# The boundary of a batch in a fused attention and feed-forward kernel: the last head pair's transpose by DMA, with other work laid behind it

## Chip, cores and metric

The kernel runs on one core of a Trainium2 chip. The metric is the device time of one execution in microseconds (us). Engines are called as in the profile: PE is TensorE (matmuls; PEld its weight loads), DVE is VectorE, ACT is ScalarE, POOL is GpSimd, SP is SyncE, whose queue issues most of the DMAs here.

## What is computed

Attention with a hash mask, and behind it a gated feed-forward block with a gated residual. Cut to what matters:

```python
# attention: batch 4, 8 heads, 768 tokens, head size 64; proj is 64 x 6
q_bits = (q @ proj > 0); k_bits = (k @ proj > 0)          # 6 bits of hash
mask   = bucket(q_bits)[:, :, :, None] == bucket(k_bits)[:, :, None, :]
attn   = softmax(where(mask, q @ k.T / 8, -1e9))
x      = heads side by side(attn @ v)                     # 3072 x 512
# feed-forward, width 1536
ffn    = (gelu(x @ w_gate) * (x @ w_val)) @ w_out
out    = x + sigmoid(x @ w_res) * ffn
```

## The kernel before, in words

**Units.** There are four batches (`b` = 0 to 3). The eight heads of a batch are taken as four pairs (`p` counts pairs over all batches, `hp` within one, `hi` is the head in the pair). The 768 tokens are six tiles of 128.

**Slots.** Attention of one batch takes 36 slots, nine a pair. In a slot (loop at L617) PE computes scores for 1024 columns (L381) into one of two PSUM buffers with the tag "sp" (two banks each), ACT takes the exponential of them (L386), and two slots later PE multiplies them with the values (L355, "av"). When a head is done, `finish` (L299) divides by the row sums on DVE (L306, L307) and writes `x_tok`, tokens on the partitions. Every head from the second batch on starts with a preset: a memset on DVE (`opened`, L321), one small matmul (`preset`, L329) and a copy on DVE (`repeat`, L333). Slot numbers for those three are at L512 to L516.

**Feed-forward of the batch.** It needs `x` with features on the partitions (`x_sb`), in four blocks of 128 features, one per pair. `finish` turns most pairs by a DMA transpose that SP issues (L310). The last pair of each batch (and the last two of the first batch) is turned on PE by `x_turn` (L335): six transposes through an identity matrix (L339) and a copy out of PSUM. `gate_val` (L404) then runs 12 blocks of hidden features; for each it makes eight matmuls with `wg` and eight with `wv` (L400: four blocks `kk` of `x`, each as 512 and 256 columns), a Gelu on ACT (L419) and a product on DVE (L420, into `hh`). The two "sp" buffers hold the two sums. In the first batch alone the sums of block 0 are begun over three pairs before the fourth pair is turned (`begun`).

**The output rows.** `project(b)` (L426) is a generator: for each of six token tiles four matmuls with `wr` (L432, PSUM tag "r", Tanh on ACT), twelve with `wo` (L446, PSUM tag "f"), two DVE instructions (L450, L453) and the store (L455). It is run a step (one matmul) at a time between the scores and the values of the next batch's slots. L624 sets the pace: 3 steps ahead, and `NMM - HELD` = 96 - 13 = 83 steps done by the last slot. The 13 that are held back run at the end of the batch (L641 to L645): four before the last values, five behind them, then `x_turn`, then the rest.

**The hash of the next batch.** `hashed` (L518) computes the hash products of two pairs, q and k, in fp32 (L205, PSUM tag "r"), `tokens` transposes them on DVE, `bits` writes the signs, and `turn` (L248) sends the result through a DMA transpose on SP. For the second and third batch `hashed` runs whole in `gate_val` after block 0 (L589); for the first it runs in two parts, three quarters behind `x_turn` and a quarter behind block 0 (L416, L639).

**What orders the work.** The program is written in the order in which each engine is to run it, and nothing reorders it. Each engine takes its own instructions in that order, and so does SP's queue. Work is attached by hand: `side_pe` and `side_work` to slots, `gv_work` to blocks of `gate_val`. A PSUM or SBUF buffer with a tag is handed to its next user when all that used it before are done.

Of the kernel before, what the change touches and what calls it, by code (L numbers as in the profile page):

```python
# [10 lines left out]
BF16 = mybir.dt.bfloat16  # L11
# [6 lines left out]
def kernel(  # L18
# [12 lines left out]
    nc = tc.nc  # L31
    B, H, S, D = q.shape
# [3 lines left out]
    P = 128  # L36
    KM = DMODEL // P
    KF = DFF // P
    T = S // P
    HP = H // 2  # L40
# [15 lines left out]
    hh_pool = ctx.enter_context(tc.tile_pool(name="hh", bufs=1))  # L56
# [242 lines left out]
    def finish(p, hi):  # L299
        b, hp = divmod(p, HP)  # L300
        if hp == 0 and hi == 0:
            x_tok[b] = x_pool.tile([P, HP, T, 2 * D], BF16, tag="x_tok", name="x_tok")
            x_sb[b] = x_pool.tile([P, HP, T, P], BF16, tag="x_sb", name="x_sb")
        o = av.pop((p, hi))
        rec = sm_pool.tile([P, T], FP32, tag="rec", name="rec")
        nc.vector.reciprocal(rec, o[:, 0:T, D])  # L306
        nc.vector.tensor_mul(x_tok[b][:, hp, :, hi * D:(hi + 1) * D], o[:, 0:T, 0:D],  # L307
                             rec.unsqueeze(2).to_broadcast([P, T, D]))
        if hi == 1 and hp < HP - (2 if b == 0 else 1):
            nc.sync.dma_start_transpose(out=x_sb[b][:, hp],  # L310
                                        in_=x_tok[b][:, hp].rearrange("p t n -> p (t n)"))

# [20 lines left out]
        nc.vector.tensor_copy(o[:, 0:T, :], o[:, T:T + 1, :].to_broadcast([P, T, D + 1]))  # L333

    def x_turn(b, hp):  # L335
        pt = mm_ps.tile([P, T, P], BF16, tag="f", name="pt") if b == 0 else \
            sc_ps.tile([P, T, P], BF16, tag="sp", name="pt")
        for t in range(T):
            nc.tensor.transpose(pt[:, t, :], x_tok[b][:, hp, t, :], ident)  # L339
        if b == 0 and hp == HP - 1:  # L340
            nc.scalar.activation(x_sb[b][:, hp, 0:2], pt[:, 0:2], AF.Copy)
            nc.vector.tensor_copy(x_sb[b][:, hp, 2:T], pt[:, 2:T])
        else:
            nc.vector.tensor_copy(x_sb[b][:, hp], pt)
# [46 lines left out]
    hidden = {}  # L391
# [9 lines left out]
                                 start=(kk == 0), stop=(kk == KM - 1))  # L401
        return sp

    def gate_val(b, begun=None):  # L404
        hh = hh_pool.tile([P, KF, S], BF16, tag="hh", name="hh")
        hidden[b] = hh
        for m in range(KF):
            ps = []
            for i, w in enumerate((wg, wv)):
                if m == 0 and begun:  # L410
                    sp = gv_mm(b, m, w, KM - 1, KM, begun[i])
                else:
                    sp = gv_mm(b, m, w, 0, KM)
                ps.append(sp)
                if m == 0 and begun and i == 1:
                    hashed((HP, HP + 1), 3, 4)  # L416
                if w is wg:
                    gt = g_pool.tile([P, S], BF16, tag="gt", name="gt")
                    nc.scalar.activation(gt, sp[:, 0:S], AF.Gelu)  # L419
            nc.vector.tensor_mul(hh[:, m, :], gt, ps[1][:, 0:S])  # L420
            for piece in gv_work.pop((b, m), []):
                piece()

# [2 lines left out]
    def project(b):  # L426
        hh = hidden[b]
        for t in range(T):
            last = b == B - 1 and t == T - 1
            rps = mm_ps.tile([P, DMODEL], FP32, tag="r", name="rps")  # L430
            for kk in range(KM):
                nc.tensor.matmul(rps, x_sb[b][:, kk, t, :], wr[:, kk, :],  # L432
                                 start=(kk == 0), stop=(kk == KM - 1))
                if kk == KM - 1:
                    th = g_pool.tile([P, DMODEL], FP32, tag="th", name="th")
                    nc.scalar.activation(th, rps, AF.Tanh, scale=0.5)  # L436
                yield
            o = o_pool.tile([P, DMODEL], FP32, tag="o", name="o")
            for k0, k1 in ((0, 3), (3, 4)) if last else ((0, KM),):
                cs = slice(k0 * P, k1 * P)  # L440
                if b < B - 1:
                    fps = mm_ps.tile([P, DMODEL], FP32, tag="f", name="fps")
                else:
                    fps = sc_ps.tile([P, DMODEL], FP32, tag="sp", name="fps")
                for m in range(KF):
                    nc.tensor.matmul(fps[:, cs], hh[:, m, bass.ts(t, P)], wo[:, m, cs],  # L446
                                     start=(m == 0), stop=(m == KF - 1))
                    if m < KF - 1:
                        yield
                nc.vector.scalar_tensor_tensor(o[:, cs], th[:, cs], 1.0, fps[:, cs],  # L450
                                               op0=ALU.add, op1=ALU.mult)
                o3 = o[:, cs].rearrange("p (k n) -> p k n", n=P)
                nc.vector.scalar_tensor_tensor(o3, o3, 0.5, x_tok[b][:, k0:k1, t, :],  # L453
                                               op0=ALU.mult, op1=ALU.add)
                nc.sync.dma_start(out_t[b, t][:, cs], o[:, cs])  # L455
            yield

# [30 lines left out]
    NSLOT = HP * NCH  # L490
    LAST = NPAIR * NCH
    LAG = 2
    HELD = 13
    AHEAD = 3
    side_pe, side_work = {}, {}

# [6 lines left out]
    def gv(b, m, *pieces):  # L503
        gv_work.setdefault((b, m), []).extend(pieces)
# [5 lines left out]


    for p in range(HP, NPAIR):  # L512
        for hi, s in enumerate((9 * p - 1, 9 * p + 4)):
            at(s - 2, lambda p=p, hi=hi: opened(p, hi))
            pe(s, lambda p=p, hi=hi: preset(p, hi))
            at(s, lambda p=p, hi=hi: repeat(p, hi))  # L516

    def hashed(ps, i0=0, i1=4):  # L518
        jobs = [(p, side) for p in ps for side in range(2)]
        for i in range(i0, i1):  # L520
            hash_mm(jobs, (i % 2,), (i // 2,))
# [55 lines left out]
    for b in range(B - 1):  # L577
        s0, p0 = b * NSLOT, (b + 1) * HP
        xs = [(p0 + i, side) for i in range(2) for side in range(2)]
        ys = [(p0 + 2 + i, side) for i in range(2) for side in range(2)]  # L580
        for j, (x, y) in enumerate(zip(xs, ys)):
            at(s0 + 24 + 2 * j, lambda x=x: tr(*x))
            at(s0 + 25 + 2 * j, lambda x=x: cast(*x, nc.gpsimd))
            if j < 2:
                at(s0 + 32 + 2 * j, lambda y=y: tr(*y))
            loads(s0 + (6 if b == 0 else 2) + 4 * j, (x[0], "qk"[x[1]]))
            loads(s0 + (22 if b == 0 else 18) + 3 * j, (y[0], "qk"[y[1]]))
        if b > 0:
            gv(b, 0, lambda p0=p0: hashed((p0, p0 + 1)))  # L589
        gv(b, 0, lambda p0=p0: tokens((p0, p0 + 1), True))  # L590
        for m, x in zip((0, 1, 2, 4), xs):
            lay(b, m, x)
        gv(b, 3, lambda y=ys[2]: tr(*y))
        gv(b, 5, lambda y=ys[3]: tr(*y))
        for m, y in zip((5, 5, 6, 6), ys):
            gv(b, m, lambda y=y: cast(*y, nc.gpsimd))
        gv(b, 6, lambda p0=p0: hashed((p0 + 2, p0 + 3)))
        gv(b, 7, lambda p0=p0: tokens((p0 + 2, p0 + 3), True))
        for m, y in zip((7, 8, 9, 10), ys):
            lay(b, m, y)  # L600
# [7 lines left out]
    def mlp_mm(n):  # L608
        while mlp and n > 0:
            try:  # L610
                next(mlp[0])
                n -= 1
                done[0] += 1
            except StopIteration:
                mlp.pop(0)

    for s in range(LAST):  # L617
        p, c = divmod(s, NCH)
        b, slot = divmod(s, NSLOT)
        cur = scores(p, c)  # L620
        for piece in side_pe.pop(s, []):
            piece()
        if b >= 1:
            mlp_mm(AHEAD + (slot + 1) * (NMM - HELD - AHEAD) // NSLOT - done[0])  # L624
        pending.append(cur)
        while len(pending) > LAG:
            values(*pending.pop(0))
        for piece in side_work.pop(s, []):
            piece()
        if slot == NSLOT - 1:  # L630
            begun = None
            values(*pending.pop(0))
            if b == 0:
                nc.scalar.activation(table, warm[:, 0:1], AF.Gelu)
                begun = [gv_mm(0, 0, wg, 0, KM - 1)]
                values(*pending.pop(0))
                begun.append(gv_mm(0, 0, wv, 0, KM - 1))
                x_turn(b, HP - 1)
                hashed((HP, HP + 1), 0, 3)  # L639
            else:  # L640
                mlp_mm(4)  # L641
                flush()
                mlp_mm(5)
                x_turn(b, HP - 1)
                mlp_mm(NMM)  # L645
            done[0] = 0
            gate_val(b, begun)
            mlp.append(project(b))
    assert not side_pe and not side_work and not gv_work
    for _ in mlp[0]:  # L650
# [31 lines left out]
```

## Time and profile before

| | |
|---|---|
| median of 3 runs | 346.91 us (346.67 to 347.25) |
| profiled execution, its own time | 346.94 us |
| its span, first to last instruction | 345.2 us |
| PE busy | 334.8 us, 97% |
| ACT, DVE, POOL busy | 206.6, 192.7, 86.0 us |
| DMA | 42.5 MB, mean 123 GB/s |
| granted TensorE clock | 1.0 |

How to read the profile. A timeline line has the start in us from the span's beginning, the duration, engine, line of the code, operation, what it writes and reads, shape and count; lines that follow each other and are alike are merged. "Idle before" in brackets is how long the engine had nothing to do, with what released it. Matmuls are pipelined and each record's end is modelled, so a matmul's cost to PE is the distance from its start to the next one's start, which is less than the duration in the record. Some matmul records are missing (a merged line with x7 where eight must be). Stretches of this profile: the first batch's attention ends at about 47 us, the slots of the second, third and fourth batch lie at about 84 to 126, 164 to 206 and 244 to 286 us, and each is followed by its `gate_val`; the last batch's output rows end the span.

### The profile page before, as it was taken

Reading aid. Unit: us, or ns where it says so; the run is one execution under the profiler, and the core shown is the slowest. Engines: PE = TensorE matmul, PEld = TensorE weight load, DVE = VectorE, ACT = ScalarE, POOL = GpSimd, SP = SyncE. Lnnn points to the kernel's source line nnn. Section 1 sums busy time; section 2 is a strip of 40 time slices with the busy share of each in tenths; the row PEclk is TensorE's granted clock in tenths of the full one; section 3 lists DMA queues with packets and bytes.
Section 4 is the critical chain, followed back from the end, with each engine's and each line's share of the span. In section 5 each row is a group of like instructions: output and inputs, shape, how many; then the busy total and the mean of one; then the engine's idle time right before and its main releaser. Section 6 shows DMA issues by size and latency. Waiting matters only on the chain.

```text
span 345.2 us, 7578 instructions
## 1 busy us (share of the span) xinstructions
PE 334.8 (97%) x3076; PEld 204.8 (59%) x3124; DVE 192.7 (56%) x405; ACT 206.6 (60%) x231; POOL 86.0 (25%) x162
## 2 busy tenths in 40 slices
PE   7999999999999999999999999999999999999995
PEld 4667665655666655555666665556566665656443
DVE  6877757755343965757345675747344445343343
ACT  3889973226999962224999992222898994323220
POOL 4779940344055000260054100143030000000000
PEclk9999999999999999999999999999999999999999
DMA  7929999949567623427467542725431221000012
GB/s 237 375 49 238 250 265 196 156 80 227 145 142 225 186 85 78 92 47 139 102 160 211 191 103 84 137 48 92 92 89 43 55 55 61 3 0 0 32 62 91
DMA packets 69572, 42.50 MB, mean 123 GB/s; under 512 B 47905, under 2 KB 66593, under 8 KB 69537
## 3 DMA queue, kind: packets, MB, share of 16 engines
q1 hardware_dynamic: 63120, 36.77, 41.4%
q0 software_dynamic: 6336, 5.24, 10.1%
q8 instruction: 24, 0.39, 0.5%
q14 instruction: 12, 0.09, 0.1%
q10 hardware_dynamic: 80, 0.00, 0.0%
HBM read 29.36 MB, written 6.29 MB: 103 GB/s over the span
## 4 chain that ended last, share of the span: by engine, by line
PE 90%; ACT 4%; DVE 2%; issue 1%; DMA 1%; SPq 0%; DVEq 0%; ACTq 0%
PE sp L400 36%; PE fps L446 17%; PE sp L381 16%; PE av L355 9%; PE rps L432 6%; ACT e L386 4%; PE hs L205 3%; PE pt L259 2%; DMA ld<-in_q_dram 1%; DVE nat L224 0%; PE pt L339 0%; PE hs L234 0%; DVE ht L215 0%; PE av L329 0%; DVE o L453 0%
## 5 line engine op out<-in xcount | busy, mean ns | idle before, releaser
L386 ACT ACTIVATE e<-sp 128x1024 bf16<-128x1024 f32 x144 | 143.8, 1027 | 14.9 <-PE sp L381 9.7
L419 ACT ACTIVATE gt<-sp 128x768 bf16<-128x768 f32 x48 | 38.9, 810 | 95.2 <-PE sp L400 95.2
L381 PE MATMUL sp<-aug,aug 71*128 71x256 bf16 (+1 forms) x384 | 86.1, 325 | 1.1 <-ACT e L386 0.6
L446 PE MATMUL fps<-wo,hh 128*128 128x512 bf16 (+2 forms) x277 | 74.2, 369 | 0.9
L420 DVE TENSOR_TENSOR hh<-gt,sp 128x768 bf16<-128x768 bf16 x48 | 45.8, 954 | 52.4 <-PE sp L400 50.9
L400 PE MATMUL sp<-x_sb,wg 128*128 128x256 bf16 (+1 forms) x374 | 69.9, 325 | 0.6
L355 PEld LDWEIGHTS <-e 128*128 128x128 bf16 x1152 | 53.3, 97 | 28.9 <-issue 1.2
L400 PE MATMUL sp<-x_sb,wv 128*128 128x512 bf16 (+1 forms) x375 | 69.9, 325 | 0.5
L355 PE MATMUL av<-va,e 128*128 128x65 bf16 x1152 | 58.7, 193 | 0.2
L400 PEld LDWEIGHTS <-wg 128*128 128x128 bf16 x384 | 37.0, 98 | 26.3 <-issue 2.1
L400 PEld LDWEIGHTS <-wv 128*128 128x128 bf16 x384 | 37.6, 98 | 24.8
L446 PEld LDWEIGHTS <-hh 128*128 128x128 bf16 x300 | 27.5, 97 | 23.2
L381 PEld LDWEIGHTS <-aug 71*128 71x128 bf16 x384 | 29.4, 97 | 10.9 <-issue 2.2
L281 POOL TENSOR_TENSOR v<-ldv 128x384 f32<-128x384 f32 x16 | 16.0, 998 | 66.2 <-DMA ldv<-in_v_dram 66.0
L184 POOL TENSOR_SCALAR nat<-ld 128x768 bf16<-128x768 f32 (+1 forms) x16 | 13.0, 810 | 75.7 <-DMA aug<-nat 73.7
L194 DVE STREAM_TRANSPOSE t<-ld 128x768 f32<-128x768 f32 (+1 forms) x34 | 30.8, 913 | 1.2 <-DMA ld<-in_q_dram 1.2
L450 DVE SCALAR_TENSOR_TENSOR o<-th,fps 128x512 f32<-128x512 f32 (+2 forms) x25 | 16.6, 665 | 24.8 <-PE fps L446 19.1
L432 PE MATMUL rps<-wr,x_sb 128*128 128x512 bf16 x90 | 26.8, 378 | 0.5
L306 DVE RECIPROCAL rec<-av 128x6 f32<-128x6 f32 x32 | 6.1, 192 | 34.8 <-PE av L355 31.1
L333 DVE COPY av<-av 128x390 f32<-128x390 f32 x24 | 13.5, 564 | 19.2 <-PE av L329 19.1
L436 ACT ACTIVATE th<-rps 128x512 f32<-128x512 f32 x24 | 14.3, 594 | 16.5 <-PE rps L432 16.5
L224 DVE TENSOR_SCALAR nat<-htp 32x72 bf16<-32x72 f32 x96 | 21.9, 229 | 1.8
(61 smaller groups left out, 205.9 us busy)
## 6 DMA issues: line engine op xcount, KB each, us to landing
ldv<-in_v_dram SPq DMA_DIRECT2D x16, 384.0 KB, 5.3
out_dram<-o SPq DMA_DIRECT2D x23, 256.0 KB, 2.1
ld<-in_q_dram SPq DMA_DIRECT2D x15, 384.0 KB, 5.3
ld<-in_k_dram SPq DMA_DIRECT2D x15, 384.0 KB, 5.1
wg<-in_moe_w_gate_dram POOLq DMA_DIRECT2D x4, 384.0 KB, 7.8
wv<-in_moe_w_val_dram POOLq DMA_DIRECT2D x4, 384.0 KB, 9.7
wo<-in_moe_w_out_dram POOLq DMA_DIRECT2D x3, 512.0 KB, 6.3
wr<-in_moe_w_res_dram POOLq DMA_DIRECT2D x1, 512.0 KB, 12.7
```

The source lines that it names most:

```text
L194: nc.vector.transpose(t32[p, side][:, sl].rearrange("p c h n -> p (c h n)"), raw[p, side][:, sl].rearrange("p c d -> p (c d)"))
L224: engs[a % len(engs)].tensor_scalar(nat_of(x)[32 * a:32 * a + 32, :, D:D + NBITS], ht[32 * j:32 * j + 32, :, NBITS * a:NBITS * (a + 1)], 0 ...
L281: nc.gpsimd.tensor_add(v3, vs[:, :, 0:3, :], vs[:, :, 3:6, :])
L355: nc.tensor.matmul(av[p, hi][:, qt, :], e[:, off:off + P], va[:, hi, jt, 0:D + 1], start=first, stop=(p >= HP and jt == T - 1), skip_group ...
L381: nc.tensor.matmul(sp[:, off:off + nq * P], ks[0:KA, hi * T + jt, :], qs[0:KA, hi * T + qt0:hi * T + qt0 + nq, :], start=True, stop=True)
L386: nc.scalar.activation(e, sp, AF.Exp, scale=float(ALPHA))
L400: nc.tensor.matmul(sp[:, c0:c1], w[:, kk, bass.ts(m, P)], xs[:, kk, c0:c1], start=(kk == 0), stop=(kk == KM - 1))
L419: nc.scalar.activation(gt, sp[:, 0:S], AF.Gelu)
L420: nc.vector.tensor_mul(hh[:, m, :], gt, ps[1][:, 0:S])
L432: nc.tensor.matmul(rps, x_sb[b][:, kk, t, :], wr[:, kk, :], start=(kk == 0), stop=(kk == KM - 1))
L446: nc.tensor.matmul(fps[:, cs], hh[:, m, bass.ts(t, P)], wo[:, m, cs], start=(m == 0), stop=(m == KF - 1))
L450: nc.vector.scalar_tensor_tensor(o[:, cs], th[:, cs], 1.0, fps[:, cs], op0=ALU.add, op1=ALU.mult)
```

## The change

Five edits belong together.

1. For the second and third batch the last pair, too, is turned by the DMA transpose in `finish`; `x_turn` is left for the first batch and the last.
2. Block 0 of `gate_val` is begun over three pairs in every batch (12 of its 16 matmuls).
3. 16 steps of `project` are held back instead of 13, which is one whole output row, and the generator's steps are cut differently: the two DVE instructions and the store of a row now come with the first step of the next row, not with the row's last step. At the end of the second and third batch the order is: four steps, the last values, the 12 begun matmuls, the other 12 steps, half of the next hash, the rest of block 0's gate sum, the rest of its value sum, the other half of the hash. In the last batch, which has no next hash, `x_turn` stands behind the 12 begun matmuls, then nine steps, the rest of block 0 and three steps.
4. `x_turn` writes into the PSUM buffer "r" in the last batch, and its copy is shared between ACT and DVE there.
5. Presets move by one slot: 9p instead of 9p - 1 for a pair that is not the first of its batch, and 9p + 5 instead of 9p + 4 for the second head.

```diff
@@ finish
-        if hi == 1 and hp < HP - (2 if b == 0 else 1):
+        if hi == 1 and (0 < b < B - 1 or hp < HP - (2 if b == 0 else 1)):
             nc.sync.dma_start_transpose(out=x_sb[b][:, hp],
@@ x_turn
-        pt = mm_ps.tile([P, T, P], BF16, tag="f", name="pt") if b == 0 else \
-            sc_ps.tile([P, T, P], BF16, tag="sp", name="pt")
+        pt = mm_ps.tile([P, T, P], BF16, tag="f" if b == 0 else "r", name="pt")
...
-        if b == 0 and hp == HP - 1:
+        if hp == HP - 1:
@@ gate_val
-    def gate_val(b, begun=None):
-        hh = hh_pool.tile([P, KF, S], BF16, tag="hh", name="hh")
-        hidden[b] = hh
+    def gate_val(b, begun, beside):
...
-                if m == 0 and begun:
+                if m == 0:
                     sp = gv_mm(b, m, w, KM - 1, KM, begun[i])
...
-                if m == 0 and begun and i == 1:
-                    hashed((HP, HP + 1), 3, 4)
+                if m == 0 and i == 1:
+                    beside()
...
+            if m == 0:
+                hidden[b] = hh_pool.tile([P, KF, S], BF16, tag="hh", name="hh")
@@ project
-                    if m < KF - 1:
-                        yield
+                    yield
...
-            yield
@@
-    HELD = 13
+    HELD = 16
@@
-        for hi, s in enumerate((9 * p - 1, 9 * p + 4)):
+        for hi, s in enumerate((9 * p - (p % HP == 0), 9 * p + 5)):
@@
-        if b > 0:
-            gv(b, 0, lambda p0=p0: hashed((p0, p0 + 1)))
@@ end of a batch
             values(*pending.pop(0))
+            ps = (HP * (b + 1), HP * (b + 1) + 1)
             if b == 0:
...
             else:
                 mlp_mm(4)
                 flush()
-                mlp_mm(5)
-                x_turn(b, HP - 1)
-                mlp_mm(NMM)
+                begun = [gv_mm(b, 0, w, 0, KM - 1) for w in (wg, wv)]
+                if b < B - 1:
+                    mlp_mm(NMM)
+                    hashed(ps, 0, 2)
+                    gate_val(b, begun, lambda: hashed(ps, 2, 4))
+                else:
+                    x_turn(b, HP - 1)
+                    mlp_mm(HELD - 7)
+                    gv(b, 0, lambda: mlp_mm(NMM))
+                    gate_val(b, begun, lambda: mlp_mm(3))
```

More of the change, by code (lines that the diff above doesn't have):

```diff
@@ L419, in gate_val @@
                     nc.scalar.activation(gt, sp[:, 0:S], AF.Gelu)
-            nc.vector.tensor_mul(hh[:, m, :], gt, ps[1][:, 0:S])
+            if m == 0:
+                hidden[b] = hh_pool.tile([P, KF, S], BF16, tag="hh", name="hh")
+            nc.vector.tensor_mul(hidden[b][:, m, :], gt, ps[1][:, 0:S])
             for piece in gv_work.pop((b, m), []):
@@ L630 @@
         if slot == NSLOT - 1:
-            begun = None
             values(*pending.pop(0))
+            ps = (HP * (b + 1), HP * (b + 1) + 1)
             if b == 0:
@@ L638 @@
                 x_turn(b, HP - 1)
-                hashed((HP, HP + 1), 0, 3)
+                hashed(ps, 0, 3)
+                gate_val(b, begun, lambda: hashed(ps, 3, 4))
             else:
@@ L642 @@
                 flush()
-                mlp_mm(5)
-                x_turn(b, HP - 1)
-                mlp_mm(NMM)
+                begun = [gv_mm(b, 0, w, 0, KM - 1) for w in (wg, wv)]
[8 more added lines that the diff above has]
+                    gate_val(b, begun, lambda: mlp_mm(3))
             done[0] = 0
-            gate_val(b, begun)
             mlp.append(project(b))
```

## The prediction

> **What bounds the kernel now.** First the busy shares and the slices, then what PE waited for, then PE's timeline at the ends of the batches.
>
> ```profile
> PE 334.8 (97%) x3076; PEld 204.8 (59%) x3124; DVE 192.7 (56%) x405; ACT 206.6 (60%) x231; POOL 86.0 (25%) x162
> ...
> PE   7999999999999999999999999999999999999995
> ...
> PEclk9999999999999999999999999999999999999999
> ```
>
> PE is full from the second slice on, at full clock. PE's waits come to four lines, all in the first 47 us; asked for the stretch from 84 us to the end, the view is empty. That view passes over short gaps, so I went through the distances between matmul starts: 216 ns after a 512-column matmul, 108 after 256 columns, 29 in a row of "av". From 84 us on only three gaps are longer for a reason other than a missing record: 0.12 us before the preset at 108.92, 0.14 us before the one at 189.14 (both wait for the memset that stands on DVE behind a row's two instructions), and 0.08 us before `x_turn` at 207.76. So the time is the sum of what PE is given, and only 0.34 us of stalls are there to be removed. This is the end of the second batch:
>
> ```profile
> 125.28 0.38 PE L432 MATMUL rps<-wr,x_sb 128*128 128x512 bf16 x1
> 125.50 0.81 PE L446 MATMUL fps<-wo,hh 128*128 128x512 bf16 x3
> 126.14 0.41 PE L355 MATMUL av<-va,e 128*128 128x65 bf16 x8
> 126.39 1.24 PE L446 MATMUL fps<-wo,hh 128*128 128x512 bf16 x5
> 127.47 0.50 PE L339 MATMUL pt<-ident,x_tok 128*128 128x128 bf16 x6
> 127.80 1.03 PE L446 MATMUL fps<-wo,hh 128*128 128x512 bf16 x4
> 128.66 1.46 PE L400 MATMUL sp<-x_sb,wg 128*128 128x512 bf16 x8
> 129.96 1.46 PE L400 MATMUL sp<-x_sb,wv 128*128 128x512 bf16 x7
> 131.36 1.51 PE L205 MATMUL hs<-t,projw 128*32 128x192 f32 x32
> 132.80 0.39 PE L400 MATMUL sp<-x_sb,wg 128*128 128x512 bf16 x1
> ```
>
> Read starts, not durations: the five matmuls at 126.39 cover exactly the time in which DVE makes `x_tok` (it ends at 127.38); nothing is lost here that the change could fill.
>
> **Removed: twelve transposes.** In the lines above the six cost 127.80 - 127.47 = 0.335 us, 56 ns each. Twice that is 0.67 us, and with them goes the 0.08 us wait at 207.76. DVE's copies (L344, 0.56 us) go as well, which is worth nothing: DVE is free there.
>
> **Added: the hash in two pieces.** Whole, as above, it costs PE 94 ns to begin (131.36 less the last matmul's start, 131.155, and its 109 ns), and 1.44 us until 132.80. The first batch shows pieces: three quarters from 50.09 to 51.21, so 1.115 us for six of eight rounds, 0.163 us a round within a piece. The end of a piece costs more, 0.25 us between the last round and the next bf16 matmul. Half a hash is 1.115 - 2 x 0.163 = 0.79, and 0.09 to begin: 0.88. Two halves are 1.77 against 1.53: 0.23 us more, twice: **0.46 us**. This is a real price, since PE has no idle time to hide it.
>
> **Moved at no price on PE.** The 12 begun matmuls, the held-back steps and the presets are the same matmuls elsewhere, with the same distances. Three steps fewer per batch in the slots shorten these by 0.65 us (3 x 0.216) and lengthen the end by as much. ACT doesn't come to limit the slots: when it is behind, its exponentials follow each other in 0.91 us (between 84 and 88 us), and the shortest slot is 1.11 us. The later presets remove the two waits, 0.26 us: for the second head of the third pair, DVE's row now begins early in slot 21 (0.8 us in) and ends with the memset 2.3 us in, and the preset runs 2.9 us in. I laid out all slots in this way. The tightest are `repeat` in slot 14 behind a row's two instructions (ready 0.4 us ahead of its values) and the preset of slot 35 (its memset 0.45 us ahead). If such a cover is gone the price is some tenths of a us a batch. A row's two instructions leave PSUM "f" late by a step, but the four "r" steps of the next row (0.86 us) and a slot of scores and values lie ahead of its next use.
>
> **Added: the transpose on SP.** On its queue it stands behind the store of the fifth row and the load of v, and ahead of the sixth row's store and of the hash's transposes, which come 3 us and more later; nothing late hangs on it but `x_sb`. Its start: in the second batch the last values end 0.65 us sooner, at 125.74; DVE is then just through the fifth row (two instructions of 0.69, from 124.48 to 125.86), so L306 and L307 run from 125.95 to 126.73; SP followed such an end by 0.08 us in this trace. Issue at 126.81. What covers it: 1.95 us of begun matmuls (12, 0.325 a pair), 12 x 0.216 = 2.59 of steps, 0.88 of hash: PE asks for the fourth pair at 125.74 + 5.42 = 131.16. So the transpose has **4.35 us** to land.
>
> ```profile
> x_sb<-x_tok SPq DMA_TRANSPOSE x11, 4.2
> ...
> DMA to landing us min/median/max: 2.7/4.2/6.3
> ```
>
> The first number is the median from issue to landing, the second line the spread. The issues at 257.20, 267.66 and 278.16, with no load about them, took 2.7 to 2.8, and so did that at 187.36; the longer ones had loads just before them (that of 117.82, 5.4, behind a k load at 117.30). Here the v load is issued by 123 and lands in 3.4 (the row at 125.58), at some 126; the store of 256 KB goes out at 125.9 and lands in 2.1, at 128. I take 2.8 to 3.2, landing at 129.6 to 130.0, and keep 2.7 and 5.4 as ends: no stall, or 1.05 us a batch.
>
> The Trainium skill, VectorE: DVE Perf Modes, sections "The three transpose paths" and "Rules for kernel authors", speaks against this edit: 390 ns for a 128x128 transpose on TensorE, 1309 on the DMA's crossbar, and TensorE is to be used where PSUM is a good place for the result. By these figures six tiles would be an estimated 2.3 us on PE and 7.9 by DMA, the removal would save 4.7 us and the transposes would come 3.5 us late, twice. The trace has 0.335 us and 2.7 to 5.4 us for the six, and the measurement decides.
>
> **The waits in block 0.** Gelu's turn decides when PE may begin block 1. In the first batch, from the end of the gate sum at 51.54 to block 1's first matmul at 52.60, it took 1.06 us with PE waiting. In the second and third batch PE has 0.33 + 0.88 = 1.21 us to do in that time: no wait. In the last batch it has 0.33 + 3 x 0.216 = 0.97: **0.09 us lost**. The table that Gelu needs is loaded well ahead (126.31 to 127.59 in the second batch); in the last batch the new copy on ACT (0.38) may stand before that load (1.28), and still both end 0.6 us before Gelu's data. There DVE's share of the copy waits for ACT's, as at 50.62 in the first batch: both are through in 1.2 us, and nine steps (1.94 us) cover them. DVE's chain in block 0 (L420 0.95, L215 0.60, four L224 0.23 each) ends 0.5 us before its next product.
>
> **Sum**, against the profiled execution of 346.94 us (span 345.2 and 1.7 around it): -0.67 - 0.08 - 0.26 + 0.46 + 0.09 = **-0.46 us**. That execution lies 0.03 above the median of the runs, so 346.91 - 0.46 = **346.45**, -0.13%. About 0.2% (0.7 us) is what a measurement can tell from no change, and I forecast less than that.
>
> **Rivals.**
>
> *The transpose is late.* It decides from 4.35 us between issue and landing, or if DVE ends `x_tok` late. For it: the median of 4.2 is close. Against it: the rows above 4.2 had other loads in the queue, and here the last one is done. At 5.4 us: 2 x 1.05 = 2.1 more, 348.5; at 4.8, half of a us a batch, 347.4. Slower.
>
> *The begun matmuls wait for the transpose.* They stand behind it in the program and read another part of the same tile. Were the order kept by whole tiles, PE would wait from 125.74 to 129.6: 3.9 us a batch, 354.2. Against it: `x_tok` was written at 28.12 (L307) while a transpose that reads another pair of that tile (issued 22.51) landed only at 28.80.
>
> *The edits cost less than I count.* If the second piece of the hash is nearly free and Gelu's turn is hidden, only the gains are left: 0.67 + 0.08 + 0.26 = 1.0 us, 345.9. Against it: the 0.25 us at the end of each piece stands at every hash of the trace.
>
> *The DMA replaces nothing in effect.* If the presets wait again, at other slots, the sum is -0.67 - 0.08 + 0.46 + 0.09 = -0.2: 346.7, inside the forecast.
>
> **Chances.** The forecast with its small variants (346.1 to 346.9) has 0.64; the late transpose 0.13; the begun matmuls held 0.03; the cheaper edits 0.17; unforeseen waits in the slots 0.03, up to 1 us a batch. From these: faster by over 0.2% (below 346.2) 0.25, within 0.2% 0.62, slower 0.13. The range of 345.8 to 347.4 takes in the forecast, the gains alone, and the transpose half a us late.
>
> **What would show it.** In the changed profile: no L339 at the ends of the second and third batch; 16 + 16 records of L205 there with four matmuls between them, each piece 0.88 us; the first fourth-pair matmul starting right at the end of the first piece; landings of 2.7 to 3.2; a gap of 0.09 before block 1 in the last batch; no gap before presets. I am wrong if PE's waits list a DMA `x_sb`, if block 0's first matmuls start 3 us after the last values, or if a gap appears at a `repeat`.

## The result

The changed kernel takes 347.40 us (median of 22 runs, 346.84 to 348.05), the kernel before 347.06 in the same session (22 runs, 346.27 to 347.32). The ratio is 1.0014, 95% interval 1.0007 to 1.0020: a small loss where a small gain was forecast. The profiled execution of the changed kernel took 347.61 us with a span of 345.9.

The end of the second batch on PE, changed kernel (start, duration, engine, line, what is written and read, count; compare the ten lines in the prediction):

```profile
125.29 0.41 PE L354 MATMUL av<-va,e 128*128 128x65 bf16 x8
125.54 1.14 PE L399 MATMUL sp<-x_sb,wg 128*128 128x512 bf16 x6
126.51 1.14 PE L399 MATMUL sp<-x_sb,wv 128*128 128x512 bf16 x6
127.49 2.75 PE L445 MATMUL fps<-wo,hh 128*128 128x512 bf16 x12
130.17 0.86 PE L205 MATMUL hs<-t,projw 128*32 128x192 f32 x16
130.96 0.50 PE L399 MATMUL sp<-x_sb,wg 128*128 128x512 bf16 x2
131.29 0.49 PE L399 MATMUL sp<-x_sb,wv 128*128 128x512 bf16 x2
131.71 0.86 PE L205 MATMUL hs<-t,projw 128*32 128x192 f32 x16
```

and SP's queue in the same place:

```profile
125.64 0.36 SPq L453 DMA_DIRECT2D out_dram<-o  x1
126.55 1.22 SPq L310 DMA_TRANSPOSE x_sb<-x_tok  x1
```

Every start follows from the one before: no wait in this stretch. The transpose of 126.55 landed 2.75 us later, at 129.30; PE asked for it at 130.96. What the change was written to do, it does. So the loss lies elsewhere, and it is found by cutting the span at PE's own marks: a batch's slots (from its first score matmul to its last "av"), the rest of the batch (from there to the last matmul of `gate_val`), and the end (from the last matmul with `wo` to the end of the span). They are worked out from the traces, in us, from start to start of matmuls. The first column is a difference, what the prediction's own sum says of changed less before; the others are lengths. The second profile is that of the first experiment below:

| stretch | forecast change | before | changed | changed, second profile |
|---|---|---|---|---|
| slots, second batch | -0.77 | 43.61 | 42.85 | 42.85 |
| rest, second batch | +0.54 | 36.48 | 37.04 | 37.04 |
| slots, third batch | -0.79 | 43.63 | 43.34 | 42.85 |
| rest, third batch | +0.46 | 36.57 | 37.04 | 37.04 |
| slots, fourth batch | -0.65 | 43.47 | 42.82 | 42.82 |
| rest, fourth batch | +0.74 | 33.40 | 34.48 | 34.46 |
| end | 0 | 4.30 | 4.63 | 4.67 |

All that the prediction priced is there to within some 0.02 us. Two lines are off in both profiles, the rest of the last batch by 0.33 and the end by 0.35; a third, the slots of the third batch, in one profile and not in the other. The first 48 us, where loads come in, differ by 0.5 us between the two profiles of the changed kernel alone and are left out.

**The last batch.** Products of `gate_val` on DVE before:

```profile
299.70 0.95 DVE L420 TENSOR_TENSOR hh<-gt,sp 128x768 bf16<-128x768 bf16 x1 [1.65 <-PE sp L400]
302.30 0.95 DVE L420 TENSOR_TENSOR hh<-gt,sp 128x768 bf16<-128x768 bf16 x1 [1.65 <-PE sp L400]
```

and in the changed kernel, with the PE matmul that waits for the second one:

```profile
302.28 0.95 DVE L419 TENSOR_TENSOR hh<-gt,sp 128x768 bf16<-128x768 bf16 x1 [1.65 <-PE sp L399]
305.25 0.95 DVE L419 TENSOR_TENSOR hh<-gt,sp 128x768 bf16<-128x768 bf16 x1 [2.02 <-PE sp L399]
306.26 1.46 PE L399 MATMUL sp<-x_sb,wv 128*128 128x512 bf16 x8 [0.18 <-DVE hh L419]
```

Products come every 2.60 us, this one after 2.97. The wait that stands before it on DVE's sequencer had ended at 304.84; in the blocks around it the product starts 0.045 us after the end of that wait, here 0.41. PE's distance at 306.26 is 0.35 us too long. POOL has no work in this part.

**The end.** After the last store SP waits for everything that is still open, two semaphores an instruction, some 0.06 to 0.07 us for each instruction, in an order that is the same in all traces. SP's loads, stores and transposes take eight completion semaphores in turn. Before, the last store had the seventh in the order and landed at 343.82, with one instruction of those waits left behind it. In the changed kernel, two DMAs on, it has the first in the order: it landed at 344.14 and seven more instructions of waits stood behind it, until 345.00. SP's waits for stores from 342 us on, before and changed (us in total, times, longest):

```profile
SPq L677 <- DMA out_dram<-o: 0.7, 2, 0.6
```

```profile
SPq L679 <- DMA out_dram<-o: 1.1, 1, 1.1
```

Before, SP stops at the last two stores one after the other, late in the order; in the changed kernel it stops once, at the head of the order.

### The profile page after: what moved, and what is told of

It reads as the page before. It is cut to its first block, busy times and chain, and to the rows that moved or that the text cites. A ratio compares the mean times of both kernels' runs of the same rounds, so it can differ in the third digit from the quotient of the medians.

```text
span 345.9 us, 7597 instructions
## 1 busy us (share of the span) xinstructions
PE 337.9 (98%) x3112; PEld 204.4 (59%) x3112; DVE 191.5 (55%) x403; ACT 206.9 (60%) x232; POOL 86.1 (25%) x162
## 4 chain that ended last, share of the span: by engine, by line
PE 89%; ACT 5%; DVE 3%; issue 1%; DMA 1%; SPq 0%; DVEq 0%; ACTq 0%
PE sp L399 36%; PE fps L445 18%; PE sp L380 15%; PE av L354 8%; PE rps L431 5%; ACT e L385 4%; PE hs L205 3%; PE pt L259 2%; DMA ld<-in_q_dram 1%; DVE o L451 1%; DVE o L448 1%; DVE nat L224 0%; PE hs L234 0%; DVE ht L215 0%; DVE hh L419 0%
## 5 line engine op out<-in xcount | busy, mean ns | idle before, releaser
L445 PE MATMUL fps<-wo,hh 128*128 128x512 bf16 (+2 forms) x300 | 79.5, 370 | 0.0
L399 PE MATMUL sp<-x_sb,wg 128*128 128x512 bf16 (+1 forms) x384 | 71.0, 326 | 0.1
L399 PE MATMUL sp<-x_sb,wv 128*128 128x512 bf16 (+1 forms) x384 | 70.9, 326 | 0.2 <-DVE hh L419 0.2
L448 DVE SCALAR_TENSOR_TENSOR o<-th,fps 128x512 f32<-128x512 f32 (+2 forms) x25 | 16.6, 666 | 36.6 <-PE fps L445 32.0
L184 POOL TENSOR_SCALAR nat<-ld 128x768 bf16<-128x768 f32 (+1 forms) x16 | 14.1, 884 | 76.8 <-DMA aug<-nat 73.0
L451 DVE SCALAR_TENSOR_TENSOR o<-o,x_tok 128x512 f32<-128x512 f32 (+2 forms) x25 | 18.2, 727 | 0.9
```

The costliest lines, as they stand in the source:

```text
L399: nc.tensor.matmul(sp[:, c0:c1], w[:, kk, bass.ts(m, P)], xs[:, kk, c0:c1], start=(kk == 0), stop=(kk == KM - 1))
```

## The experiments

Times are medians; "before" was run beside each of them (346.98 to 347.05).

**The changed kernel again.** No edit.

> The changed kernel, unaltered. Theory: its trace is longer than the sum of the prediction in three places, and all of them come back in a second profile: the third batch's slots hold some 0.5 us of PE stalls (an 'av' that waits for a late repeat, a preset that waits for a late memset, each behind a row's second DVE instruction that POOL's work lengthens to 1.3 us), the last batch's gate_val one stall of some 0.35 us, and from the last matmul with wo to the end of the span it takes 4.63 us instead of 4.30. Time against the kernel before: +0.3 to +0.6 us. Rival (the extra is scatter of one execution): the stalls lie elsewhere or are gone, and the last stretch is 4.3 us again.

347.41 us, ratio to before 1.0008 (0.9998 to 1.0017). The stall at 306.28 (0.33 us) and the long end are back. The third batch's two stalls are not: 42.85. So two of the three belong to the program and one to the execution.

**Two small DMAs added to the kernel before.**

```diff
+    for s in (37, 73):
+        at(s, lambda: nc.sync.dma_start(spare, proj.rearrange("(h r) n -> r h n", r=32)))
```

> The kernel before with two more small DMAs on SP (1.5 KB each, in slots of the second and third batch). Theory: SP's DMAs take eight completion semaphores in turn, the end of the program waits for them in a fixed order, and the changed kernel's two additional transposes moved the last store's from late in that order to its first place, so that the other waits stand behind the last landing. Then two more DMAs of any kind give the same: the stretch from the last matmul with wo to the end grows from 4.30 to some 4.6 us, +0.3 us in the time, nothing else changes. Rival: the longer end has to do with the changed end of the last batch or with code; then the stretch stays at 4.30.

The end grew from 4.30 to 4.64, as expected, with nothing else changed at the end of the program. The time is 347.23, ratio 1.0000 (0.9991 to 1.0008), where 0.3 us more would be 1.0009: the times of whole runs don't confirm it here, the trace does. The third batch's slots show 0.44 us of stall before a preset, three times that of the first profile of before: this stall varies in the old kernel too.

**Six small DMAs added to the changed kernel.** The same edit, slots 37, 39, 41, 73, 75, 77.

> The changed kernel with six more small DMAs on SP in the slots of the second and third batch, so that the last store again takes the seventh of the eight completion semaphores, as in the kernel before. Theory (the order of the final waits): the stretch from the last matmul with wo to the end of the span falls from 4.63 to 4.30 us, 0.33 us less time than the changed kernel. Rival (the end belongs to the changed program in another way): it stays at 4.6.

The last store has the seventh semaphore again, and the end is 3.88 us: 0.75 less than in the changed kernel, where 0.33 was expected. Time 346.57, ratio to before 0.9987 (0.9978 to 0.9996). The rest is a pause of SP's. Between two of its instructions at the end it stands idle for 0.35 to 0.36 us, where 0.03 to 0.06 is usual: in before from 343.98 to 344.34, in the changed kernel from 344.48 to 344.83, in the kernel with two DMAs from 344.65 to 345.01. In each of the ten traces that have it, the pause stands ahead of SP's 208th recorded instruction (its waits counted). With six more DMAs the 208th is the store ahead of the last, for which SP waits 2.15 us anyway, and no pause is left behind the last landing. So the order of the waits is confirmed, as about half of what the six DMAs gained.

**One and two DVE instructions added to the changed kernel.**

```diff
+    for s in (113,):          # and (113, 116)
+        at(s, lambda: nc.vector.memset(spare_v, 0.0))
```

> The changed kernel with one more DVE instruction (a memset of one element a partition, a slot of the last batch). In all changed kernels DVE's 448th instruction, the product of block 5 in the last gate_val, starts 0.40 us after the wait before it has ended, PE stands 0.33 us for it, and the fetch of 8 KB of code follows 0.65 us after its start; in the kernel before the same fetch follows an instruction that nobody waits for. Theory: DVE steps from one piece of its code to the next there, between the wait and the product. One instruction more moves the step ahead of the wait, where it is hidden: the stall of PE goes, 0.33 us less. Rival (something else of the last batch delays this product, such as its place behind the row's instructions): the stall stays.

> The changed kernel with two more such DVE instructions. Waits and products alternate in DVE's code there, so by the theory the step falls between a wait and a product again, one block earlier: PE's stall of 0.33 us is back, at block 4, and the time is that of the changed kernel. Rival (a delay bound to the block or to the time): it stays at block 5, or it is gone with any added instruction.

With one more, the product of block 5 has its 1.65 us of idle time like all others; no PE stall is left in `gate_val` but Gelu's (0.09), and the rest of the fourth batch takes 34.13:

```profile
304.48 0.95 DVE L420 TENSOR_TENSOR hh<-gt,sp 128x768 bf16<-128x768 bf16 x1 [1.65 <-PE sp L400]
```

With two more, the late product is back one block earlier, and PE's stall with it (34.48):

```profile
302.04 0.95 DVE L420 TENSOR_TENSOR hh<-gt,sp 128x768 bf16<-128x768 bf16 x1 [2.02 <-PE sp L400]
...
303.05 0.48 PE L400 MATMUL sp<-x_sb,wv 128*128 128x512 bf16 x2 [0.18 <-DVE hh L420]
```

In each trace with a late product it is DVE's 448th recorded instruction (waits counted) that comes late. Times 346.99 (1.0001, 0.9992 to 1.0010) and 347.06 (1.0001, 0.9993 to 1.0010); the second was expected at the changed kernel's 347.4, and the runs don't separate the two. The traces do: from the second batch's first score matmul to the end of the span it is 262.75 us in the changed kernel's second profile, 262.37 with one more instruction and 262.72 with two; what else these two profiles are shorter by lies ahead of that stretch. What is shown is that the delay is bound to a place in DVE's code and not to a block, and that it costs nothing where that place lies ahead of a wait. That the place is a step between pieces of code is inferred, not shown: in the changed kernel an 8 KB instruction fetch begins at 305.90, 0.65 us after the late product's start, and in before one at 300.76, 0.1 us behind the end of DVE's 447th instruction, which a long wait follows.

**The hash in one piece.**

```diff
                 if b < B - 1:
                     mlp_mm(NMM)
-                    hashed(ps, 0, 2)
-                    gate_val(b, begun, lambda: hashed(ps, 2, 4))
+                    gate_val(b, begun, lambda: hashed(ps))
```

> The changed kernel with the next hash in one piece behind block 0's sums in the second and third batch. The transpose is then covered by 1.95 + 2.59 = 4.54 us behind the last values: it landed 3.76 us behind them, so PE shouldn't wait. Theory: a piece of hash costs 0.23 us of PE for its beginning and end; the time falls by 0.46 us against the changed kernel. Rival: the pieces cost nothing, or the transpose or Gelu's turn makes PE wait here; then the time stays or rises, with a gap at the fourth pair's first matmul or before block 1.

```profile
128.19 2.75 PE L445 MATMUL fps<-wo,hh 128*128 128x512 bf16 x12
130.78 0.49 PE L399 MATMUL sp<-x_sb,wg 128*128 128x512 bf16 x2
131.10 0.49 PE L399 MATMUL sp<-x_sb,wv 128*128 128x512 bf16 x2
131.52 1.51 PE L205 MATMUL hs<-t,projw 128*32 128x192 f32 x32
132.96 0.71 PE L399 MATMUL sp<-x_sb,wg 128*128 128x512 bf16 x3
```

The fourth pair's matmul at 130.78 follows its predecessor without a gap, and the rest of the second and third batch take 36.80, 0.24 less each. Time 346.94, 0.47 below the changed kernel beside it, ratio to before 0.9998 (0.9988 to 1.0008). A piece of hash costs what was forecast, and the first half was not needed as cover.

**The transposes on PE again.**

```diff
-        if hi == 1 and (0 < b < B - 1 or hp < HP - (2 if b == 0 else 1)):
+        if hi == 1 and hp < HP - (2 if b == 0 else 1):
...
                 if b < B - 1:
+                    x_turn(b, HP - 1)
                     mlp_mm(NMM)
```

Two of the small DMAs, in slots 37 and 73, stand in for the two transposes on SP's queue.

> The changed kernel with one part undone: in the second and third batch the last pair is turned by six transposes on PE again (behind the 12 begun matmuls, PSUM buffer r, copy shared by ACT and DVE) and not by the DMA transpose. Two small DMAs on SP take the places of the two transposes in the turn of the completion semaphores. Theory: the DMA transpose is hidden altogether, so what it is worth is the six transposes, 0.33 us a batch: from the last 'av' to the last matmul of gate_val 37.37 us instead of 37.04, and some 0.7 us more in the time. Rival (the DMA transpose costs something elsewhere, on SP's queue or in the slots): the difference is smaller than 0.5 us, and the slots of the second or third batch are shorter here.

37.38 in the rest of both batches, 0.34 more than in the changed kernel. Time 348.53, ratio to before 1.0040 (1.0027 to 1.0052); some 1.1 us over the changed kernel's 347.4 of the other sessions, more than expected: 0.67 of it are the transposes; the profile also has stalls of 0.13 and 0.25 us in the slots, which vary; the rest is not accounted for. By the trace the DMA transpose is hidden and worth its six matmuls.

**The presets' slots, undone and alone.** In the changed kernel `enumerate((9 * p - 1, 9 * p + 4))`; in the kernel before `enumerate((9 * p - (p % HP == 0), 9 * p + 5))`.

> The changed kernel with the presets, memsets and repeats in their slots of before (9p - 1 and 9p + 4). Theory: the new slots put them on DVE right behind a row's two instructions (rows 1 and 2), in the old slots they stand ahead of these or a slot and more behind; so the third batch's two stalls (0.23 and 0.28 us) go, and the time falls by 0.4 to 0.5 us against the changed kernel, to the kernel before or 0.1 below it. Rival: the late steps of the rows are to blame and not the presets' slots; then stalls of the same size stand at other presets and the time stays.

> The kernel before with the new slots of presets, memsets and repeats alone. Theory: alone they take the preset that waited for a row (0.12 to 0.44 us in a batch) away from right behind it, 0.2 to 0.5 us less than the kernel before. Rival: in the old pace of the rows another preset or repeat comes to stand behind a row, and the time stays or rises.

Both theories fell. PE's waits for DVE in the slots, from 84 us on, first of the changed kernel with the old slots, then of the old kernel with the new slots:

```profile
PE av L329 <- DVE av L321: 1.0, 3, 0.3
```

```profile
PE av L355 <- DVE av L333: 2.5, 3, 0.8
```

349.04 (ratio to before 1.0058, 1.0045 to 1.0071) and 349.41 (1.0073, 1.0061 to 1.0086). This view leaves out short idle times and counts from the modelled end of a matmul; the distances between starts show more. In the first, presets wait for memsets that now stand behind a row: 0.51 and 0.31 us in the second batch, 0.49 and 0.31 in the third, 0.49 in the fourth. In the second, once a batch PE waits almost 1 us for a repeat that stands on DVE behind a row which itself waits for PE. The new pace of the rows and the new slots of the presets are one edit; neither stands alone.

**Without POOL's work in the third batch.** The casts are skipped for b > 0, and `vaug` and `vsums` of the third and fourth batch are those of four pairs earlier.

> The changed kernel without POOL's work for the third and fourth batch: the values, their sums and the casts of q and k are left out there (older tiles are used in their place), so that its output isn't the reference's. Theory: a row's second DVE instruction takes 0.69 us wherever POOL does nothing and up to 1.36 beside POOL, and that alone makes the stalls of the third batch's slots, which differ from one profile to the next (0 to 0.5 us). Then all rows of the third batch take 0.69 here and its slots hold no stall: 42.85 us from the last gate_val matmul to the last 'av', as in the best of the profiles. Rival (the stalls come from the order on DVE or from late loads): rows above 0.8 us or stalls remain.

An output row's two DVE instructions in slot 14 of the third batch (L451 is the second), in the changed kernel's first profile, then in its second, then here:

```profile
178.68 0.69 DVE L448 SCALAR_TENSOR_TENSOR o<-th,fps 128x512 f32<-128x512 f32 x1 [2.16 <-ACT e L385]
179.40 1.30 DVE L451 SCALAR_TENSOR_TENSOR o<-o,x_tok 128x512 f32<-128x512 f32 x1
180.63 0.56 DVE L333 COPY av<-av 128x390 f32<-128x390 f32 x1
```

```profile
179.93 0.69 DVE L451 SCALAR_TENSOR_TENSOR o<-o,x_tok 128x512 f32<-128x512 f32 x1
180.54 0.56 DVE L333 COPY av<-av 128x390 f32<-128x390 f32 x1
```

```profile
179.18 0.69 DVE L451 SCALAR_TENSOR_TENSOR o<-o,x_tok 128x512 f32<-128x512 f32 x1
```

In the first profile POOL's next instruction (L184) is long as well, 1.23 where 0.82 is usual:

```profile
179.34 0.82 POOL L273 CAST va<-ldv 128x768 bf16<-128x768 f32 x1
180.10 0.15 POOL L274 MEMSET va<- 128x12 bf16 x1
180.17 1.23 POOL L184 TENSOR_SCALAR nat<-ld 128x768 bf16<-128x768 f32 x1
```

In the second profile, where the row took 0.69, POOL's L184 beside it took 1.25: there POOL alone was held up. Without POOL's work every row of the third batch takes 0.69, its slots hold no stall and take 42.85. That alone would not tell, since the second profile has no stall either; the sizes do. Over the other profiles with the changed kernel's slots the row of slot 14 or 21 in that batch takes 0.69 to 1.36, and the PE stall follows it: none at 1.05 and below, 0.03 at 1.09, 0.13 at 1.20, 0.23 at 1.30, 0.25 at 1.32 and 0.28 at 1.34 and 1.36. The time, 346.96, ratio 0.9999 (0.9989 to 1.0008), isn't used: work is missing, and SP's code ends at its 204th instruction, without the pause (end 4.25). So the third stall is DVE and POOL in each other's way, and its size depends on how the two happen to lie.

**All together.** The whole hash; four steps instead of three behind block 0's sums in the last batch; the six DMAs; the one memset.

> All together: the changed kernel with the hash in one piece behind block 0 (second and third batch), one step of the output rows moved behind block 0's sums in the last batch (four instead of three, against the 0.09 us that PE waits for Gelu), six small DMAs that turn the semaphores, and one DVE instruction. Theory: the four gains add up, 0.46 + 0.09 + 0.33 + 0.33 = 1.2 us less than the changed kernel, some 0.8 to 0.9 us less than the kernel before (346.1 to 346.2). Rival (the gains are covered by one another or by the scatter of the slots): less than 0.5 us below the kernel before.

345.61 us, ratio to before 0.9953 (0.9941 to 0.9966): 1.4 us less than the kernel before, more than expected, since the end gave 0.77 and not 0.33. The rest of the last batch took 34.04: 0.33 from DVE's place and 0.09 from Gelu's turn. The third batch's slots even had a stall of 0.28 in its profile.

## Why the prediction was wrong

Its steps in their order:

- *PE is the bound, and the time is the sum of what it is given.* Right for all stretches but two: one stall of 0.33 us on PE in the last batch, and what stands behind the last matmul.
- *Twelve transposes, 0.335 us a batch.* Right: 0.34, by undoing.
- *The hash in two pieces, 0.23 us each.* Right: 0.24, by undoing.
- *The transpose lands at 129.6 to 130.0, PE asks at 131.16.* Right in what follows, no wait: issued at 126.55 for 126.81, it took 2.75 us, a little under the 2.8 to 3.2, and landed at 129.30; PE asked at 130.96. (The view's spread went to 6.3, for an issue in the first batch, and not only to the 5.4 that the text kept as its end.)
- *Gelu's turn in the last batch, 0.09.* Right: the distance is 0.305 instead of 0.216, and one more step took it away.
- *The later presets remove the waits of 0.12 and 0.14.* Right for the second batch in both profiles, for the third in one of two. The covers were worked out with 0.69 for a row's second instruction, while the page's group for that line had a mean of 0.75 and single rows of 0.97 to 1.21 beside POOL. The cover of `repeat` in slot 14, "ready 0.4 us ahead", was gone whenever the row took 1.3. This is the "some tenths of a us" that the text put on it, and the text's own sign of being wrong, a gap at a `repeat`, stands in the first profile (0.23 us at 181.24, and 0.28 at the preset of 190.10) and not in the second. It makes scatter, in both kernels, and not the verdict: over the second and third batch the slots' stalls come to 0 to 0.49 us, 0.19 in the mean, in the eight profiles with the changed kernel's slots and all of POOL's work, and to 0.26 and 0.44 in the two with the old ones.
- ***"Nothing late hangs on it but `x_sb`"***: this failed. Two more DMAs on SP's queue shift all later ones in the turn of eight semaphores, and the end of the program waits by them: 0.35 us. The sum took the 4.30 us behind the last matmul as a constant; it was 4.63 and 4.67.
- ***The sum of the last batch*** had only Gelu's 0.09. It took the products on DVE to follow their waits at once, as they do before (0.045 us). The changed count of DVE's instructions put a delay of 0.37 us between a wait and its product: 0.33 to 0.35 us on PE. The first of the two failed terms was put at nothing without a look at the end of the program, the second is not mentioned at all.

The forecast of -0.46 and these two terms make +0.2, and +0.4 with the mean stall that is left in the slots; the measured difference is +0.3 (0.2 to 0.7 by the interval). None of the rivals was it: the transpose was not late, the begun matmuls did not wait, and the edits cost just what was counted. That the measured 347.40 lies at the upper end of the stated range is chance, since that end was set for a transpose half a us late. The side of the answer was lost on two terms that have nothing to do with what the change is for. With changes of 0.1%, such terms are as large as the change.

## What to carry to other kernels

Where one engine is full, as PE is here, a sum of its matmuls can hold to hundredths of a us, so look for the error in what was taken as constant: the stretch behind the last matmul, and the time between a wait and the instruction that it releases. Before you judge an edit of some tenths of a us, take the span apart at marks of the bound engine and set aside what an added idle instruction or DMA would move as well. Take an instruction's duration from its slowest rows when another engine works beside it, and move work that shares an engine's order together.

## What the runs showed of the hardware that was not expected

An engine can stand still at a fixed place of its code: 0.37 us ahead of DVE's 448th recorded instruction, 0.35 us ahead of SP's 208th, whichever instruction that is. For DVE an 8 KB instruction fetch begins 0.65 us after the late product's start (changed kernel). The Trainium skill, Runtime: NRT & Kernel Launch, section "Instruction fetch mechanics", says that code streams in by blocks and that crossing to the next is mostly hidden. That the delay is such a crossing is inferred here. Whatever it is, it is hidden where the engine waits anyway; between a wait and the work it releases it cost PE 0.33 us.

A DVE instruction with two SBUF inputs (L451) takes 0.69 us beside an idle POOL and 0.69 to 1.36 beside a busy one, by how the two lie; the one with an input in PSUM (L448) took 0.68 to 0.69 in these kernels throughout. The Trainium skill, SBUF — State Buffer, section "SBUF: two separate sides", states just this: DVE instructions with two SBUF inputs and POOL's share a pair of ports that one of them holds for a whole instruction. The rows agree: in the second profile the row is short and POOL's L184 long, in the first both are long. A sum that counts on 0.69 beside POOL goes wrong by it.

The end of this program waits for its DMAs' semaphores in a fixed order, at some 0.06 to 0.07 us for two; which semaphore the last store happens to have was worth 0.3 us (4.30 to 4.64 by two added DMAs).
